# A score tile inside two dense chunks, the sums of one norm ahead of two casts, one turn of x sooner

## The chip, the cores and the metric

The kernel runs on one core of a Trainium2 chip. The metric is device time of one execution in microseconds (us). The core has a matrix engine (TensorE, PE; its weight loads are PEld), a vector engine (DVE), an activation engine (ScalarE, ACT), a general engine (GpSimd, POOL) and a sync engine (SP) that here only issues DMA. Each works off its own instructions in the order in which the program lists them, and waits where one of them needs another engine's result.

## The reference

The program is an attention with RMS-normalised q and k, followed by a mixture of experts with a dense part. Shapes: q, k, v are 8 x 12 x 448 x 64; the tokens are 3584 x 768, 8 experts, hidden size 512.

```python
q_n, k_n = rmsnorm(q, g_q), rmsnorm(k, g_k)          # x / sqrt(mean(x*x) + 1e-6) * g
attn = softmax(q_n @ k_n.T / 8); x = attn @ v        # x becomes 3584 x 768
y_dense = relu(x @ w1_dense) @ w2_dense
expert_idx = argmax(x @ w_gate); gate_w = softmax(x @ w_gate)[expert_idx]
y_moe = gate_w * (relu(x @ w1[expert_idx]) @ w2[expert_idx])
out = y_dense + y_moe
```

## The kernel before

The heads of one image are taken in three groups of four, so the attention has 24 groups g, three to an image; an image takes about 24 us, which is called a period here. For a group, DVE takes statistics of q and k (`stats`, L281), ACT squares the means (`means`, L288), POOL adds them to the sums of squares (`ss`, L290), ACT takes logarithm and exponential (`norms`, L294 and L296) and gets 1/rms as `r`. POOL multiplies q and k with it (`normalise`, L302, four instructions that write `xn`) and casts v (`values`, L267, two casts that write `va`). PE transposes `xn` into the two banks of the PSUM tile `W` (`transposes`, L313, 28 of them) and DVE copies them out (`qT`, `kT`).

Scores come in seven tiles per group (`scores`): PE multiplies into a PSUM tile `sc` (L348), of which there are two, and ACT takes the exponential (L350, an "exp"). The products with v are L366 (`AV`), and DVE divides them (L393). Once a group's x is there, PE turns it (`xtrans`, L407), DVE copies it (`xturned`, L413), and PE makes the router's logits from it (L425).

When an image's x is complete, its dense layer follows in four chunks m of 128 tokens (`dense`, L616, six matmuls each with 512 columns, the last chunk in halves) during the next period. A chunk lands in bank 0 or bank 1 of `W`, the same banks that the transposes L313 write, and ACT empties it with a relu (`relu`, L624). Its records go to memory with an indirect DMA that POOL issues (`scatter`, L488). POOL also issues the loads of the experts' weights (L680); SP issues the loads of q, k and v (L235, L261), and a load into a staging buffer waits until POOL has read what was there.

The order of all this is a table, `AT`: each step gets a time in units of a seventh of a group, `attention` sorts all steps by it, and the steps are written out in that order. A time says nothing but where a step stands among the others; on each engine the instructions run in that order. Steps from unit 161 on stand in a list of their own, `AT['tail']`, which also has the turns of gathered tokens and the loads of expert numbers into PE's registers (`number`, L847).

In the attention `s1` to `s6` are the times of the score tiles, with one entry for each of the three groups of a period; `me` is that of `means`, which puts L288 on ACT and L290 on POOL; `de` holds the dense chunks, in pieces of the six matmuls.

After the attention (from about 205 us) PE works through expert tiles, with two matmul stages each, and the outputs go out by indirect DMA.

## Time and profile before

| | us |
|---|---|
| median of 3 runs | 353.22 |
| the three runs | 355.0, 351.29, 353.22 |
| the profiled execution | 350.3 |
| its span | 348.6 |
| PE, busy (share of the span) | 312.8 (90%) |
| DVE | 231.4 (66%) |
| ACT | 212.8 (61%) |
| POOL | 202.2 (58%) |

Shares are means over the whole span. In the attention, up to about 200 us, PE, DVE, ACT and POOL are each busy for eight to nine tenths or more of most slices; after it PE alone is. [...]

### The profile page before, as it was taken

Reading aid. Unit: us, or ns where it says so; the run is one execution under the profiler, and the core shown is the slowest. Engines: PE = TensorE matmul, PEld = TensorE weight load, DVE = VectorE, ACT = ScalarE, POOL = GpSimd, SP = SyncE. Lnnn points to the kernel's source line nnn. Section 1 sums busy time; section 2 is a strip of 40 time slices with the busy share of each in tenths; the row PEclk is TensorE's granted clock in tenths of the full one; section 3 lists DMA queues with packets and bytes.
Section 4 is the critical chain, followed back from the end, with each engine's and each line's share of the span. In section 5 each row is a group of like instructions: output and inputs, shape, how many; then the busy total and the mean of one; then the engine's idle time right before and its main releaser. Section 6 shows DMA issues by size and latency. Waiting matters only on the chain. (4 is left out here: it accounts for less than half of the span.)

```text
span 348.6 us, 11328 instructions
## 1 busy us (share of the span) xinstructions
PE 312.8 (90%) x4164; PEld 192.7 (55%) x4164; DVE 231.4 (66%) x835; ACT 212.8 (61%) x348; POOL 202.2 (58%) x290
## 2 busy tenths in 40 slices
PE   0389989989989899999899899999999999999990
PEld 0255656656656565666666556555555555555550
DVE  5988998878988879888898744258222226364641
ACT  2389998898898898998988834322332332323220
POOL 4666887788886987988987522462323221322222
PEclk9999999999999999999999999999999999999997
DMA  7999999999997999989999799999999948495422
GB/s 263 265 249 240 311 291 210 289 259 323 233 305 240 256 300 253 285 227 253 262 276 192 166 186 182 259 282 248 176 248 240 212 121 205 123 182 140 123 93 80
DMA packets 83406, 78.85 MB, mean 226 GB/s; under 512 B 46894, under 2 KB 76088, under 8 KB 83344
## 3 DMA queue, kind: packets, MB, share of 16 engines
q1 hardware_dynamic: 69360, 42.58, 50.8%
q0 software_dynamic: 13984, 35.47, 40.5%
q8 instruction: 36, 0.59, 0.7%
q14 instruction: 26, 0.21, 0.2%
HBM read 61.40 MB, written 23.02 MB: 242 GB/s over the span
## 5 line engine op out<-in xcount | busy, mean ns | idle before, releaser
L350 ACT ACTIVATE xflat<-sc 128x896 bf16<-128x896 f32 x168 | 143.8, 918 | 6.0 <-PE sc L348 5.4
L302 POOL TENSOR_TENSOR xn<-we,r 128x448 bf16<-128x448 f32 x90 | 82.0, 945 | 14.5 <-issue 6.8
L348 PE MATMUL sc<-qT,kT 64*128 64x448 bf16 (+1 forms) x384 | 65.9, 372 | 12.0 <-ACT xflat L350 8.8
L366 PE MATMUL AV<-va,xflat 128*128 128x65 bf16 (+1 forms) x1536 | 75.7, 195 | 0.5 <-ACT xflat L350 0.4
L281 DVE BATCH_NORM_STATS2 st<-we 128x6 f32<-128x128 f32 x336 | 70.3, 280 | 2.9 <-DMA we<-in_k_dram 2.8
L366 PEld LDWEIGHTS <-xflat 128*128 128x128 bf16 (+1 forms) x1536 | 59.9, 98 | 22.2 <-issue 12.1
L929 POOL DMA_INDIRECT out_dram<-xflat,tail x22 | 22.7, 1032 | 64.5 <-DVE xflat L928 52.4
L928 DVE COPY xflat<-yp 128x768 f32<-128x768 f32 x22 | 21.0, 956 | 46.3 <-PE yp L898 46.3
L878 ACT COPY heT<-AV 128x512 bf16<-128x512 bf16 x26 | 15.2, 585 | 55.3 <-PE AV L874 55.3
L488 POOL DMA_INDIRECT records<-rall,slot x32 | 33.1, 1036 | 23.7 <-ACT rall L624 18.0
L616 PE MATMUL W<-wd,xT 128*128 128x512 bf16 (+1 forms) x240 | 42.8, 339 | 0.7 <-DVE kT L334 0.7
L898 PE MATMUL yp<-we,heT 128*128 (+1 forms) x232 | 42.5, 326 | 0.0
L348 PEld LDWEIGHTS <-kT 64*128 64x128 bf16 (+1 forms) x384 | 24.1, 97 | 28.3 <-issue 22.0
L393 DVE TENSOR_TENSOR rall<-AV,inv 128x256 bf16<-128x256 f32 x96 | 36.3, 420 | 1.7
L859 PE MATMUL W<-we,xflat 128*128 (+1 forms) x132 | 32.6, 379 | 0.3 <-issue 0.2
L624 ACT ACTIVATE rall<-W 128x512 bf16<-128x512 f32 (+1 forms) x40 | 20.3, 509 | 19.9 <-PE W L616 18.4
L887 PE MATMUL yp<-wd,xflat 128*128 128x384 bf16 x176 | 32.2, 327 | 0.0
L864 ACT ACTIVATE hs<-W,tail 128x512 bf16<-128x512 f32 x26 | 17.9, 687 | 23.1 <-PE W L859 19.5
L898 PEld LDWEIGHTS <-heT 128*128 128x128 bf16 (+1 forms) x304 | 22.5, 97 | 15.0 <-issue 1.0
L267 POOL CAST va<-we 128x448 bf16<-128x448 f32 x48 | 26.9, 593 | 0.0
L616 PEld LDWEIGHTS <-xT 128*128 128x128 bf16 (+1 forms) x240 | 16.8, 102 | 15.3 <-issue 4.4
L887 PEld LDWEIGHTS <-xflat 128*128 128x128 bf16 x176 | 16.9, 98 | 14.1 <-issue 1.3
(151 smaller groups left out, 348.6 us busy)
## 6 DMA issues: line engine op xcount, KB each, us to landing
we<-in_moe_w_dram POOLq DMA_DIRECT2D x16, 768.0 KB, 10.0
we<-in_q_dram SPq DMA_DIRECT2D x24, 448.0 KB, 9.6
we<-in_k_dram SPq DMA_DIRECT2D x11, 896.0 KB, 8.2
we<-in_v_dram SPq DMA_DIRECT2D x48, 128.0 KB, 9.6
we<-in_v_dram SPq DMA_DIRECT2D x48, 96.0 KB, 7.2
wd<-in_moe_w_dense_dram POOLq DMA_DIRECT2D x2, 768.0 KB
we<-in_k_dram SPq DMA_DIRECT2D x2, 448.0 KB, 3.5
records<-rall,slot POOLq DMA_INDIRECT x32, 6.6
```

The source lines that it names most:

```text
L267: nc.gpsimd.tensor_copy(vas[g % 3][:, :, :, a * 32:a * 32 + 32].rearrange("p s h i -> p h s i"), xin["v", g].rearrange("p h (s i a) -> p h ...
L281: return [lambda s=s: nc.vector.bn_stats(sts[g][:, "qk".index(name), s].rearrange("p h c -> p (h c)"), xin[name, g].rearrange("p h (s d) - ...
L302: (eng or nc.gpsimd).tensor_tensor(xn[name, g][:, :, hh], xin[name, g][:, hh].rearrange("p (s d) -> p s d", d=D), r[:, "qk".index(name), : ...
L348: nc.tensor.matmul(ps[out, hh, :S], kT[row, w:w + out.stop - out.start], qT[row, r], start=True, stop=True, skip_group_check=True)
L350: nc.scalar.activation(x, ps[:, :, :S], AF.Exp, scale=scale)
L366: on("AV", nc.tensor.matmul(av[:, hh, m], exs[g, s][rows_, hh, QC[m]:QC[m] + P], va[rows_, s, hh, :De], start=(first and s == full[0] and ...
L393: on("AV", nc.vector.tensor_tensor(x[:, 2 * hh + r], av[:, hh, :, :D].rearrange("p m (a i) -> p m a i", a=2), inv[:, hh].unsqueeze(3).to_b ...
L488: i = nc.gpsimd.indirect_dma_start(out=rec, out_offset=bass.IndirectOffsetOnAxis(ap=slot[b % 2][:, m:m + 1], axis=0), in_=rb[b % 3][:, m], ...
L616: on("W", nc.tensor.matmul(o, xTs[b][:, kk, q0:QC[m] + P], wd1[:, kk, c], start=(kk == 0), stop=(kk == KD - 1), skip_group_check=(m == 3)) ...
L859: got = [nc.tensor.matmul(he[c], xRs[t][:, kk, c], matrix(t, 0, h, kk * F, (kk + 1) * F), start=(kk == 0), stop=(kk == KD - 1)) for h, c i ...
L887: nc.tensor.matmul(yps[t][:, dd, :HD], xRs[t][:, KD + i], wd2[:, i, dd * HD:(dd + 1) * HD], start=(i == 0), stop=False, skip_group_check=True)
L898: return [nc.tensor.matmul(yp[c, dd, :HD], heTs[t][:, i, c], matrix(t, 1, h, cols.start, cols.stop), start=False, stop=(i == FT - 1), skip ...
```

## The change

Three numbers of the table change, the third dense chunk is cut in two, and one step gets a time of its own.

```diff
- 'me': [2.591, 2.79, 3.569],
+ 'me': [1.6, 2.79, 3.569],
...
-        (2, 0, [(20.56, 0, 6)], 20.943, 27.29), (3, 0, [(26.48, 0, 6)], 28.824, 32.5)],
+        (2, 0, [(20.56, 0, 2), (20.62, 2, 6)], 20.943, 27.29), (3, 0, [(26.48, 0, 6)], 28.824, 32.5)],
...
  'sx': {(5, 3): 155.2},
+ 'xs': {22: 160.9},
...
- 's0': [-0.586, 0.455, 2.566],
+ 's0': [-0.586, -0.4, 2.566],
...
- 's3': [0.9, 0.991, 3.16],
+ 's3': [0.65, 0.991, 3.16],
...
- 'tail': [('tu', 0), ('tu', 1), ('tu', 2), ('nu', 0), ('nu', 1), ('xt', 22), ('de', 6, 2), ('de',
+ 'tail': [('tu', 0), ('tu', 1), ('tu', 2), ('nu', 0), ('nu', 1), ('de', 6, 2), ('de',
...
-            put1(at("xt", z, g), ("xt", g), xtrans, g)
+            put1(AT["xs"].get(g, at("xt", z, g)), ("xt", g), xtrans, g)
```

What this does to the engines' order, at the three places where it matters. Line numbers of the changed kernel are one higher from the new row of the table on.

PE, third dense chunk of the first image (a period near 64 us; `xT_81` is that image's x, `kT_92` the keys of a group, `wgb` the router's weights):

```order
L366 MATMUL AV<-va_93,xflat 128x65
L616 LDWEIGHTS xT_81
L616 MATMUL W<-wd_88,xT_81 128x512
...
L425 LDWEIGHTS xT_82
L425 MATMUL AV<-wgb,xT_82 128x8
...
L348 LDWEIGHTS kT_92
L348 MATMUL sc<-qT,kT_92 128x448
```

```order
L617 LDWEIGHTS xT_81
L617 MATMUL W<-wd_88,xT_81 128x512
L349 LDWEIGHTS kT_92
L349 MATMUL sc<-qT,kT_92 128x448
L349 LDWEIGHTS kT_92
L349 MATMUL sc<-qT,kT_92 128x448
L617 LDWEIGHTS xT_81
L617 MATMUL W<-wd_88,xT_81 128x512
```

Before, the six matmuls of the chunk stood together, and the logits and then two score tiles followed. Now two of the six come, then the first of those score tiles (two matmuls), then the other four, the logits, and the second score tile. In the second chunk likewise a score tile (the one in quarters, of four matmuls), which stood behind all six, stands behind two of them. Both hold in six periods.

ACT, first period with a dense part, from the first relu on (`m` is the square, `xflat<-sc` an exp):

```order
L624 ACTIVATE rall<-W 128x512
L350 ACTIVATE xflat<-sc 128x896 x2
L624 ACTIVATE rall<-W 128x512
L350 ACTIVATE xflat<-sc 128x896 x2
L288 ACTIVATE m_1471<-st 128x28
```

```order
L625 ACTIVATE rall<-W 128x512
L351 ACTIVATE xflat<-sc 128x896 x3
L625 ACTIVATE rall<-W 128x512
L351 ACTIVATE xflat<-sc 128x896
L289 ACTIVATE m_1471<-st 128x28
```

One exp has moved ahead of the second relu, and in the same way one moves ahead of the third; the squares keep their place among the exps.

POOL, second period with a dense part (`va_94` is the cast of v, `ss` the sum that needs ACT's square, `rall` a record):

```order
L302 TENSOR_TENSOR xn<-we,r 128x7x64 x4
L488 DMA records<-rall,slot_85 29824x648
L267 CAST va_94<-we 128x2x7x32 x2
L290 TENSOR_TENSOR ss<-st,m_2287 128x28
L488 DMA records<-rall,slot_85 29824x648
L680 DMA we<-in_moe_w_dram 128x3x1024
```

```order
L303 TENSOR_TENSOR xn<-we,r 128x7x64 x4
L489 DMA records<-rall,slot_85 29824x648
L291 TENSOR_TENSOR ss<-st,m_2256 128x28
L268 CAST va_94<-we 128x2x7x32 x2
L489 DMA records<-rall,slot_85 29824x648
L681 DMA we<-in_moe_w_dram 128x3x1024
```

The sum has moved ahead of the two casts; this holds in six groups, five of them in periods with a dense part. The fourth piece of the change, at the end of the attention, moves the eight transposes L407 of group 22 on PE from behind logits, a product `AV` and two register loads (L847) to the place ahead of these. The orders of DVE and SP are the same as before.

## Rows read from the trace of the kernel before

**Rows 1.** Table by stretch, after the attention: us, then busy time of each engine.

```profile
240.00:260.00 20.00, 20.00 (x126) 11.47 (x125) 7.02 (x20) 6.36 (x10) 5.75 (x6) 1.00 1.04 235
```

**Rows 2.** Waits of the whole run: us in total, times, longest.

```profile
ACT rall L624 <- PE W L616: 18.4, 22, 2.7
...
PE sc L348 <- ACT xflat L350: 8.8, 20, 1.0
```

**Rows 3.** Timeline of PE, period from 76 us: start, duration, [idle before <-releaser].

```profile
83.07 1.47 PE L616 MATMUL W<-wd,xT 128*128 128x512 bf16 x6
...
86.34 0.35 PE L348 MATMUL sc<-qT,kT 64*128 64x448 bf16 x1
...
89.15 1.47 PE L616 MATMUL W<-wd,xT 128*128 128x512 bf16 x6
90.46 0.34 PE L425 MATMUL AV<-wgb,xT 128*128 128x8 bf16 x8
...
92.11 0.36 PE L348 MATMUL sc<-qT,kT 64*128 64x448 bf16 x2
...
99.33 0.37 PE L348 MATMUL sc<-qT,kT 64*128 64x448 bf16 x2 [0.52 <-ACT xflat L350]
...
100.23 0.58 PE L313 MATMUL W<-ident,xn 64*128 64x64 bf16 x28 [0.24 <-POOL xn L302]
```

**Rows 4.** Timeline of PE's weight loads behind the second chunk, same period.

```profile
84.47 0.11 PEld L348 LDWEIGHTS <-kT 64*64 64x64 bf16 x4 [0.42 <-issue]
84.78 0.10 PEld L348 LDWEIGHTS <-kT 64*128 64x128 bf16 x2 [0.20 <-issue]
...
85.22 0.44 PEld L313 LDWEIGHTS <-xn 64*128 64x128 bf16 x26 [0.33 <-issue]
```

**Rows 5.** Timeline of ACT, same period.

```profile
84.58 0.60 ACT L624 ACTIVATE rall<-W 128x512 bf16<-128x512 f32 x1 [0.77 <-PE W L616]
...
86.66 0.25 ACT L288 ACTIVATE m<-st 128x28 f32<-128x28 f32 x1
86.79 0.93 ACT L350 ACTIVATE xflat<-sc 128x896 bf16<-128x896 f32 x1
...
91.15 2.53 ACT L350 ACTIVATE xflat<-sc 128x896 bf16<-128x896 f32 x3
93.55 0.26 ACT L288 ACTIVATE m<-st 128x28 f32<-128x28 f32 x1
```

**Rows 6.** Timeline of POOL, same period.

```profile
88.31 3.64 POOL L302 TENSOR_TENSOR xn<-we,r 128x448 bf16<-128x448 f32 x4 [1.07 <-ACT r L296]
...
93.18 1.14 POOL L267 CAST va<-we 128x448 bf16<-128x448 f32 x2
...
94.69 1.01 POOL L488 DMA_INDIRECT records<-rall,slot  x1 [0.17 <-issue]
...
96.50 3.67 POOL L302 TENSOR_TENSOR xn<-we,r 128x448 bf16<-128x448 f32 x4
```

**Rows 7.** Timeline of ACT, the same place one period later.

```profile
117.67 0.26 ACT L288 ACTIVATE m<-st 128x28 f32<-128x28 f32 x1
...
119.58 0.32 ACT L294 ACTIVATE ln<-ss,eps_t 128x28 f32<-128x28 f32 x1 [0.84 <-POOL ss L290]
```

**Rows 8.** Timeline of POOL there.

```profile
118.17 1.17 POOL L267 CAST va<-we 128x448 bf16<-128x448 f32 x2
...
120.74 3.64 POOL L302 TENSOR_TENSOR xn<-we,r 128x448 bf16<-128x448 f32 x4
```

**Rows 9.** Timeline of PE: the third transposes of that period and of the next.

```profile
124.94 0.58 PE L313 MATMUL W<-ident,xn 64*128 64x64 bf16 x28
...
149.19 0.58 PE L313 MATMUL W<-ident,xn 64*128 64x64 bf16 x28 [0.33 <-POOL xn L302]
```

**Rows 10.** Timeline of PE at the end of the attention.

```profile
205.31 0.62 PE L407 MATMUL W<-ident,rall 128*128 128x128 bf16 x8 [0.82 <-issue]
```

**Rows 11.** Waits of SP's DMA queue.

```profile
SPq L261 <- POOL ss L290: 14.4, 8, 4.8
```

## The prediction

> **What bounds the kernel now.** I read the table by stretch first. After the attention PE has no gap: 20.00 of 20 us [rows 1]. So whatever PE loses or gains before that point reaches the end unchanged, and only the attention has to be worked out. There the table of waits shows where the edits aim: ACT stands 18.4 us before relus, waiting for dense chunks, and PE stands 8.8 us for a score buffer that ACT has not emptied yet [rows 2]. A score tile inside the chunk gives ACT an exp to do during the first wait, and that could shorten the second.

> Next I followed one period on four engines. It closes in a ring. PE's second dense chunk and the transposes behind it set when ACT can take the next exps; behind these ACT makes the `r` of one group; that releases POOL's multiplication for this group at 88.31; from there POOL works almost without a gap through records, casts, sum, records, a weight load and the third group's multiplication, until 100.17 [rows 6]; and PE's transposes of the third group wait for that last one, 0.24 us here and 0.33 us two periods on [rows 3, 9]. I call these the third transposes. So in these periods POOL, not ACT, has the last word: PE's wait of 0.52 us for ACT at 99.33 [rows 3] costs little, since without it PE would only stand longer at the third transposes.

> **Second chunk: a tile inside it.** Before, the weight loads behind the chunk are those of the tile in quarters (84.47), of one more tile (84.78), and then of the transposes, of which the first two go through and the others are held, with a gap of 0.33 us, until 85.22 [rows 4]. The relu ran from 84.58 to 85.18 [rows 5]: it empties the bank into which the second transpose writes. So the two tiles cost PE nothing there; they fill the time in which the transposes wait for the relu.

> With the quarter tile inside the chunk, the chunk ends later, so the relu ends later, and the transposes with it. The tile itself takes 0.31 us (84.47 to 84.78) [rows 4]. To it comes the change from full-height to half-height matmuls and back. From the start of six dense matmuls to the next work it is 1.40 us where a half-height tile follows (83.07 to 84.47) and 1.31 us where full-height logits follow (89.15 to 90.46) [rows 3, 4], so one change costs 0.09 us. The way back has no row of its own; its bounds are 0 and, as for the way there, 0.09, and I take 0.09. Insertion: 0.31 + 0.18 = 0.49 us.

> [...]

> What follows from the 0.49 us: the next score pair, whose second matmul ended at 86.34 + 0.35 = 86.69, ends at 87.18, and its exp, at 86.79 before, can start at about 87.2, 0.4 us later, although ACT is there sooner [rows 3, 5]. Logarithm and exponential for `r` stand behind that exp in ACT's order. So POOL's start of 88.31 becomes 88.7, and its first records end at 93.6 instead of 93.18.

> **Third chunk: a tile inside it, and the sum ahead of the casts.** PE arrives 0.49 us later and now has two more changes of height before the score tile of 92.11, which comes at 92.11 + 0.49 + 0.18 = 92.78. The tile itself costs nothing extra, because it only changes places with the rest of the chunk. This score tile feeds the last exp before the square: it is ready at 92.78 + 0.36 = 93.14, an exp takes 0.8 us in a row of three (91.15 to 93.55), so the square starts at 93.95 and ends at 94.2, where before it ran from 93.55 to 93.81 [rows 5].

> POOL now has the sum ahead of the casts. POOL is free at 93.6, but the sum needs the square: it starts at 94.3. Before, casts (1.14), sum and a gap (0.17) took 1.51 us from 93.18 to the records at 94.69, so a sum takes 0.20 us. Everything on POOL's queue stands behind it: the casts start at 94.5, and behind them there is no sum any more, so the records come 1.14 + 0.17 us later, at 95.8 to 95.85, against 94.69: 1.15 us late [rows 6]. The weight load and the third group's multiplication follow without a gap, so the third transposes move from 100.23 by up to 1.15 us. If the square were no later than before, the sum would end at 94.15 and the records would come at 95.45, 0.75 us late. Middle of the two: **+0.95 us for this period, and the same for its twin at 149.19** [rows 9]: +1.9 us.

> **Where the sum's move is meant to help.** One period later the square (117.67 to 117.93) is there before POOL reaches the casts at 118.17, and behind casts and sum ACT stands 0.84 us before its logarithm [rows 7, 8]. That wait goes. But POOL's multiplication for the third group ends at 120.74 + 3.64 = 124.38, and comes 0.4 us later by its later start; the third transposes stand at 124.94 [rows 8, 9], so they can come at about 124.85: −0.1 us, although ACT gains more. The two remaining periods with third transposes lie between this one (−0.1) and the twins (+0.95). They do not wait for POOL today, so I take them below the middle, +0.35 each: +0.7 us.

> **The rest.** The sixth period with a dense part has no third transposes; there PE just carries the 0.49 us: +0.5. The turn of group 22 puts 0.45 us of transposes (205.31 to 205.76, when the next chunk begins) ahead of the register loads instead of behind them, and with them the gap of 0.82 us [rows 10]. What follows is ready in both cases. If the gap stays as long behind the new neighbour, nothing is won; if the loads run during the transposes, 0.45 us. I take 0, since the same 32 product instructions stand right before the loads in both orders. SP and DVE keep their orders, and each score tile, cast and sum takes as long as before.

> **Sum:** 1.9 − 0.1 + 0.7 + 0.5 + 0 = **+3.0 us**. On the profiled execution of 350.3 us that is 353.3 us. The median of the runs shown is 353.22 us, 2.9 us above the profiled execution, and the changed kernel will be judged beside such runs: **356.2 us**. With the low ends (0.75 for the twins, −0.1 for the two others, −0.45 for the turn) the sum is 1.5 − 0.1 − 0.2 + 0.5 − 0.45 = +1.25; with the high ones (1.15; 0.95 for the others) 2.3 − 0.1 + 1.9 + 0.5 = +4.6.

> **Rivals.**
> - *ACT's lead counts, POOL does not hold the transposes.* Then the two waits of rows 2 shrink as meant. Worked out: the stands for a score buffer, at most 8.8 us in all of which some 5 lie in these periods, go, and twelve insertions cost 12 × 0.18 = 2.2: about −3 us, 350.2. For it: a tenth of that 18.4 us of ACT's waiting suffices. Against it: POOL's gapless stretch of rows 6 and both waits of rows 3 and 9. Chance 0.12.
> - *Nearly nothing.* The square comes early enough that POOL does not stand, and PE's later chunks are swallowed by the waits for ACT that follow (0.52 us each period). Then only the last period's +0.5 and a few tenths remain: 353.5 to 354. For it: PE's waits are there to swallow it; against it: the square of 93.81 against POOL at 93.18 [rows 5, 6]. Chance 0.26.
> - *Worse: loads come late.* The casts empty the staging of v; SP's loads of v wait on POOL there already, 14.4 us in 8 waits [rows 11], and q and k queue behind them. If a cast 1.3 us later makes the next multiplication wait for data, five periods lose up to 1.3 us in place of the terms above: 5 × 1.3 + 0.5 = +7, 360. It decides once POOL's first multiplication waits for a load and not for `r`. Against it: SP has long idle waits. Chance 0.10.

> The forecast keeps 0.52.

> **Range and chances.** A run of this kernel varies by 1 to 2 us, so about 1% (3.5 us) is what can be told from no change: the borders are 349.7 and 356.75. Forecast and high ends reach past the upper one in some four tenths of their cases: 0.52 × 0.4 = 0.21, with the last rival 0.30 for slower. Half of the first rival and a little of the second lie below the lower one: 0.07 for faster. Within 1%: 0.63. The range takes in the second rival and the high ends with the spread of the runs: 352.0 to 358.8. Below it lies the first rival, above it the third, together about 0.2.

> **What the profile after would show.** The relu of the second chunk ends half a us later and the transposes' row behind it grows or starts later; ACT's waits before second and third relu shrink to a tenth or two. POOL has a wait "sum for square" of 0.5 to 0.8 us in at least three periods, and PE's waits at the third transposes grow from 0.24 and 0.33 to near 1 us and appear in other periods. ACT's wait before the logarithm (0.84) is gone. At the end the gap of 0.82 us stands before a dense chunk. I am wrong if the third transposes come sooner relative to the period's start, if the sum finds its square done, or if the transposes behind the second chunk are not held by its relu.

## The result, and the profile after

The changed kernel takes **356.87 us** (median of 5 runs, 355.07 to 358.94) beside 353.22 us before in the same session. The ratio is **1.0129, with a 95% interval of 1.0093 to 1.0166**, some 4.5 us; the two medians alone differ by 3.65. I had forecast 356.2 us from a sum of +3.0 us, and had given 0.63 to a change of less than 1% and 0.30 to slower. The median lies just outside that 1%, whose upper border was 356.75 us.

The profiled execution is the longest of the five: 358.94 us, span 357.2 us, mean granted clock 0.978. The one before had a span of 348.6 us and 0.993. Of these 8.6 us some 2 are thus this execution's own, and 2.9 come from the one before, which took 350.3 us against a median of 353.22. Executions that the comparison counts as disturbed are left out of every ratio below, so that two kernels (e3, e4) have a trace but no ratio, and the traces of e3, e4, e5, e8 and e9 are of such executions. In those five traces PE waits for a DMA behind the attention, once or twice for 4.4 to 7.5 us, and it is 150.5 to 161.2 us from the dense chunk that follows the attention to the end, against 142.1 to 144.1 in the other eight; up to that chunk they are held against the others below.

The table of waits after, the lines that answer to [rows 2], and POOL's and the third transposes' beside them (us in total, times, longest):

```profile
ACT xflat L351 <- PE sc L349: 18.2, 39, 1.2
...
POOL xn L303 <- ACT r L297: 12.0, 8, 2.1
ACT rall L625 <- PE W L617: 9.0, 8, 2.7
PE sc L349 <- ACT xflat L351: 6.5, 16, 0.8
...
PE W L314 <- POOL xn L303: 3.8, 5, 1.0
```

ACT's waits before its relus halved and PE's for score buffers shrank from 8.8 to 6.5 us, as the edit intends. But the time came back in other rows. ACT's waits for scores were 5.4 us before, POOL's for `r` 2.8, and PE's at transposes for POOL's product 1.3.

The second chunk of the period from 76 us on PE, to hold against [rows 3, 4]:

```profile
83.56 0.39 PE L617 MATMUL W<-wd,xT 128*128 128x512 bf16 x1
84.10 0.38 PE L349 MATMUL sc<-qT,kT 64*64 64x448 bf16 x4
84.41 1.04 PE L617 MATMUL W<-wd,xT 128*128 128x512 bf16 x4
85.38 0.36 PE L349 MATMUL sc<-qT,kT 64*128 64x448 bf16 x2
85.58 0.19 PE L314 MATMUL W<-ident,xn 64*128 64x64 bf16 x1
86.14 0.56 PE L314 MATMUL W<-ident,xn 64*128 64x64 bf16 x27 [0.36 <-issue]
```

(The second matmul of the first row has no record.) From the chunk's start to the relu it was 1.51 us [rows 3, 5]; now it is 85.49 − 83.56 = 1.93. The insertion costs 0.42 us, and the transposes stand 0.36 us for the relu. ACT at the same place, against [rows 5]:

```profile
85.49 0.60 ACT L625 ACTIVATE rall<-W 128x512 bf16<-128x512 f32 x1
85.98 0.91 ACT L351 ACTIVATE xflat<-sc 128x896 bf16<-128x896 f32 x1
86.78 0.24 ACT L289 ACTIVATE m<-st 128x28 f32<-128x28 f32 x1
87.64 0.92 ACT L351 ACTIVATE xflat<-sc 128x896 bf16<-128x896 f32 x1 [0.61 <-PE sc L349]
88.45 0.31 ACT L295 ACTIVATE ln<-ss,eps_t 128x28 f32<-128x28 f32 x1
88.79 0.23 ACT L297 ACTIVATE r<-ln 128x28 f32<-128x28 f32 x1
```

ACT is earlier at its work, but the exp at 87.64 has to wait 0.61 us for scores that PE makes 0.42 us later. The logarithm and `r` stand behind this exp in ACT's order. This wait of 0.6 us is there in all six periods. POOL behind it, against [rows 6]:

```profile
89.15 3.64 POOL L303 TENSOR_TENSOR xn<-we,r 128x448 bf16<-128x448 f32 x4 [1.80 <-ACT r L297]
...
94.51 0.24 POOL L291 TENSOR_TENSOR ss<-st,m 128x28 f32<-128x28 f32 x1 [0.51 <-ACT m L289]
94.70 1.11 POOL L268 CAST va<-we 128x448 bf16<-128x448 f32 x2
95.97 1.00 POOL L489 DMA_INDIRECT records<-rall,slot  x1 [0.16 <-issue]
96.97 0.82 POOL L681 DMA_DIRECT2D we<-in_moe_w_dram  x1
97.79 3.65 POOL L303 TENSOR_TENSOR xn<-we,r 128x448 bf16<-128x448 f32 x4
```

The sum waits 0.51 us for its square, with casts, records, weight load and the third multiplication behind it. Against the start of the second chunk the records come 12.41 us in place of 11.62, 0.79 us later. And PE at the third transposes, against the end of [rows 3]:

```profile
100.27 0.37 PE L349 MATMUL sc<-qT,kT 64*128 64x448 bf16 x2 [0.65 <-ACT xflat L351]
100.57 0.36 PE L426 MATMUL AV<-wgb,xT 128*128 128x8 bf16 x8
101.50 0.58 PE L314 MATMUL W<-ident,xn 64*128 64x64 bf16 x28 [0.57 <-POOL xn L303]
102.01 0.68 PE L349 MATMUL sc<-qT,kT 64*64 64x448 bf16 x6
102.62 2.00 PE L367 MATMUL AV<-va,xflat 128*128 128x65 bf16 x29
```

The last row took 1.39 us before (from 101.35 us). The table by stretch shows why it takes 2.00 (busy time of each engine, and behind POOL's the granted clock as a share of full speed):

```profile
100.00:101.00 1.00, 0.65 (x10) 0.36 (x9) 0.06 (x2) 1.00 (x3) 1.00 (x2) 1.00 1.01 266
101.00:102.00 1.00, 0.50 (x28) 0.47 (x28) 0.97 (x4) 0.96 (x3) 1.00 (x3) 1.00 1.11 240
102.00:103.00 1.00, 1.00 (x22) 0.59 (x17) 0.93 (x4) 0.56 (x1) 0.89 (x3) 0.90 1.09 219
103.00:104.00 1.00, 1.00 (x19) 0.82 (x17) 0.93 (x5) 1.00 (x2) 0.93 (x1) 0.50 1.13 232
...
106.00:107.00 1.00, 0.81 (x13) 0.52 (x13) 0.00 (x0) 0.92 (x2) 1.00 (x2) 0.89 0.64 217
```

Behind two stands (times in which PE idles) of 0.65 and 0.57 us the granted clock falls to 0.50 for 3.4 us (102.8 to 106.2 us); summed over the rows of the table, the two that are left out included, that is 1.71 us of clock lost. The same happens at 154 and at 205 us, for 3.4 us each. In the trace before, the granted clock is 1.00 throughout up to 343 us, and PE's last work starts at 339.15 us. What a fall costs can be read from the stretch from the third transposes to the second chunk: 6.96 us twice without one (76.60 to 83.56, 127.36 to 134.32), 8.26 and 8.20 with one. So **one fall costs about 1.25 us**, an estimate from these two. Nothing in my sum stands for it.

### The profile page after: what moved, and what is told of

The parts are those of the page before. It is cut to its first block, busy times and chain, and to the rows that moved or that the text cites. A ratio compares the mean times of both kernels' runs of the same rounds, so it can differ in the third digit from the quotient of the medians.

```text
span 357.2 us, 11293 instructions
## 1 busy us (share of the span) xinstructions
PE 313.7 (88%) x4129; PEld 194.0 (54%) x4164; DVE 231.8 (65%) x835; ACT 216.5 (61%) x348; POOL 202.2 (57%) x290
## 5 line engine op out<-in xcount | busy, mean ns | idle before, releaser
L351 ACT ACTIVATE xflat<-sc 128x896 bf16<-128x896 f32 x168 | 146.0, 916 | 19.9 <-PE sc L349 18.2
L303 POOL TENSOR_TENSOR xn<-we,r 128x448 bf16<-128x448 f32 x90 | 82.0, 943 | 18.4 <-ACT r L297 12.0
L367 PE MATMUL AV<-va,xflat 128*128 128x65 bf16 (+1 forms) x1536 | 79.0, 198 | 1.9 <-ACT xflat L351 0.4
L349 PE MATMUL sc<-qT,kT 64*128 64x448 bf16 (+1 forms) x384 | 69.0, 380 | 10.2 <-ACT xflat L351 6.5
L367 PEld LDWEIGHTS <-xflat 128*128 128x128 bf16 (+1 forms) x1536 | 62.5, 99 | 24.9 <-issue 14.3
L860 PE MATMUL W<-we,xflat 128*128 (+1 forms) x121 | 30.5, 379 | 1.5 <-issue 0.7
```

The source lines that it names most:

```text
L303: (eng or nc.gpsimd).tensor_tensor(xn[name, g][:, :, hh], xin[name, g][:, hh].rearrange("p (s d) -> p s d", d=D), r[:, "qk".index(name), : ...
L349: nc.tensor.matmul(ps[out, hh, :S], kT[row, w:w + out.stop - out.start], qT[row, r], start=True, stop=True, skip_group_check=True)
L351: nc.scalar.activation(x, ps[:, :, :S], AF.Exp, scale=scale)
L367: on("AV", nc.tensor.matmul(av[:, hh, m], exs[g, s][rows_, hh, QC[m]:QC[m] + P], va[rows_, s, hh, :De], start=(first and s == full[0] and ...
L860: got = [nc.tensor.matmul(he[c], xRs[t][:, kk, c], matrix(t, 0, h, kk * F, (kk + 1) * F), start=(kk == 0), stop=(kk == KD - 1)) for h, c i ...
```

## The experiments

The traces are compared by the third transposes of every period (P1 to P5 are the five periods from one to the next), and by the stretch from the last of them to the next dense chunk after the attention. A star marks a fall of the clock in the stretch.

| kernel | P1 | P2 | P3 | P4 | P5 | sum | sum less 1.25 per fall | last stretch |
|---|---|---|---|---|---|---|---|---|
| before | 24.93 | 24.23 | 24.71 | 24.25 | 24.14 | 122.26 | 122.3 | 32.43 |
| after | 25.18 | 24.90 | 25.86* | 25.95 | 25.57* | 127.46 | 125.0 | 34.22* |
| e1 sum alone | 25.05 | 24.79 | 25.51* | 24.89 | 24.03 | 124.27 | 123.0 | 33.73* |
| e2 second chunk alone | 25.05 | 24.56 | 25.06 | 24.59 | 24.48 | 123.74 | 123.7 | 34.18* |
| e3 third chunk alone | 25.22 | 24.22 | 24.72 | 24.26 | 24.15 | 122.57 | 122.6 | 33.89* |
| e9 turn alone | 24.72 | 24.22 | 25.15 | 24.92 | 24.24 | 123.25 | 123.3 | 32.45 |
| e5 after, sum put back | 25.04 | 24.56 | 25.07 | 24.60 | 25.70* | 124.97 | 123.7 | 32.72 |
| e4 after, r early | 25.18 | 26.35* | 24.11 | 25.01 | 24.31 | 124.96 | 123.7 | 32.12 |
| e8 before, r early | 24.41 | 24.73 | 24.41 | 24.52 | 24.39 | 122.46 | 122.5 | 32.43 |
| e7 e5, r early | 23.97 | 24.27 | 24.00 | 24.07 | 24.10 | 120.41 | 120.4 | 32.23 |
| e10 second chunk, r early | 24.51 | 24.73 | 24.28 | 24.67 | 25.04 | 123.23 | 123.2 | 34.16* |
| e11 third chunk, r early | 24.64 | 24.63 | 24.48 | 24.54 | 24.94 | 123.23 | 123.2 | 34.22* |

In P1 to P5, e9 has the order of the kernel before. Its 1.0 us more (in P3 and P4, with stands of 0.27 and 0.30 us that the trace before lacks) say how far one trace can be trusted: sums that differ by less than 1 us are not told apart by the sums alone, and what a smaller difference comes from has to be read from the rows. In e6 the third transposes stand elsewhere, so it has no row here.

**The sum alone (e1).**

```
- 'me': [2.591, 2.79, 3.569],
+ 'me': [1.6, 2.79, 3.569],
```

> Only the norms' sum of one group in three goes ahead of the two casts; PE's order stays as before. Theory A (POOL's lateness reaches PE as a stand at the third transposes): the sum waits 0.4 to 0.6 us for its square in the twin periods, the casts come behind it, and the third transposes come 0.5 to 0.8 us later there; the period with the 0.84 us wait before the logarithm gives 0.1 back: +0.5 to +1.5 us against before. Theory B (only what is put into PE's chunks costs): 0. Theory C (the whole loss is the granted clock that falls behind longer stands of PE): 0 where no stand passes half a us, else about 1.25 us for each fall.

Measured: ratio **1.0096** (1.0057 to 1.0136), some 3.4 us. POOL's wait is there, and the stands at the third transposes with it:

```profile
94.14 0.24 POOL L290 TENSOR_TENSOR ss<-st,m 128x28 f32<-128x28 f32 x1 [0.72 <-ACT m L288]
...
97.43 3.65 POOL L302 TENSOR_TENSOR xn<-we,r 128x448 bf16<-128x448 f32 x4
```

```profile
99.52 0.37 PE L348 MATMUL sc<-qT,kT 64*128 64x448 bf16 x2 [0.52 <-ACT xflat L350]
99.82 0.36 PE L425 MATMUL AV<-wgb,xT 128*128 128x8 bf16 x8
101.14 0.58 PE L313 MATMUL W<-ident,xn 64*128 64x64 bf16 x28 [0.96 <-POOL xn L302]
```

The five periods grow by 0.8 us without the fall; P2 and P4, the twins, by 0.56 and 0.64 us. That is theory A's figure, and far less than 3.4. (P4 of e9 is as long without the sum's move, so it is the rows above that show the wait, not the lengths.) The rest is the clock. The seven executions behind the ratio had lost 4.9 to 8.2 us of clock each (one less the mean granted clock, times the span; median 6.3), against 1.4 to 4.6 in the kernel before (medians of 2.6 to 3.0 in three sessions, the program's end included, where PE has nothing to do). By estimate the difference of some 3.5 us is two falls of 1.71, at 1.25 us each 2.5 us. 0.8 and 2.5 make 3.3 of the 3.4. Theory B falls. Theory C has the larger part right, but not the whole: the stands that the sum's wait makes cost time of their own.

**The tile in the second chunk alone (e2).**

```
- 's3': [0.9, 0.991, 3.16],
+ 's3': [0.65, 0.991, 3.16],
```

> Only the quarter score tile goes inside the second dense chunk, six times. Theory A: 0.42 us on PE each time, as in the changed kernel's trace; the exp that stands ahead of the logarithm on ACT then waits for its scores, so POOL's multiplication starts 0.3 us later against the chunk; stands at the third transposes of 0.3 to 0.7 us in the twins: +2.5 to +3.5 us, and 1.25 more for each fall of the clock. Theory B: 6 x 0.42 = +2.5 us, stands at the third transposes no longer than before (0.24 and 0.33). Theory C: 0, or a multiple of 1.25 us.

Measured: ratio 1.0038 (0.9998 to 1.0079), median loss of clock 2.5 us, as before. The five periods grow by 1.5 us, and the last stretch by 0.5 beside its fall: 2.0 us of waits, against 1.3 measured, whose interval reaches from 0 to 2.8 us.

```profile
100.36 0.37 PE L348 MATMUL sc<-qT,kT 64*128 64x448 bf16 x2 [0.53 <-ACT xflat L350]
100.65 0.36 PE L425 MATMUL AV<-wgb,xT 128*128 128x8 bf16 x8
101.22 0.58 PE L313 MATMUL W<-ident,xn 64*128 64x64 bf16 x28 [0.21 <-POOL xn L302]
```

The stands at the third transposes are 0.21 and 0.24 us, where they were 0.24 and 0.33. POOL's multiplication starts 0.35 us later against the second chunk, but PE arrives later by as much (0.33 us). So theory B is right for this edit, though not in its size of 2.5 us: PE pays for it itself, 0.33 to 0.35 us in each of P2 to P5.

**The tile in the third chunk alone (e3).**

```
- (2, 0, [(20.56, 0, 6)],                  's0': [-0.586, 0.455, ...
+ (2, 0, [(20.56, 0, 2), (20.62, 2, 6)],   's0': [-0.586, -0.4, ...
```

> Only the score tile goes inside the third dense chunk, six times (and the tile ahead of the logits in the turns without a chunk). All theories: 0.05 us on PE each time, as in the changed kernel's trace, +0.3 us. Theory A adds that ACT's exps before the square of the third group come earlier, which POOL, late by itself, does not use: -0.3 to +0.5 us against before. If ACT's lead counts, -1 to -2 us.

Measured: no ratio. In the trace the five periods grow by 0.3 us, but not as expected: all of it is in P1, and P2 to P5 are within 0.01 us of before. No wait shrinks either: PE still stands 0.52 us for ACT ahead of the third transposes in each.

**The changed kernel with r early (e4).**

```
- 'no': [3.342, 3.796, 4.041],
+ 'no': [3.342, 3.796, 3.691],
```

> The changed kernel, and on ACT the logarithm and the exponential for r of one group in three go ahead of the one exp that waits 0.6 us for its scores there; nothing else moves. Theory A: POOL's multiplications start some 0.8 us earlier in every period, the stands at the third transposes (0.96, 0.57, 0.48 and 0.93 us) shrink to 0.3 or less, and the falls of the granted clock behind them go: 3 to 5.5 us less than the changed kernel, -1 to +1.5 us against before. Theory B: as the changed kernel, +4 to +5 us against before. Theory C: 1.25 us less for each fall that goes, at most 3.75 us less than the changed kernel.

Measured: no ratio. The trace shows half of it. POOL's multiplication starts 1.06 us sooner against the second chunk, and yet the third transposes stand:

```profile
88.78 3.64 POOL L303 TENSOR_TENSOR xn<-we,r 128x448 bf16<-128x448 f32 x4 [0.74 <-ACT r L297]
...
95.19 0.24 POOL L291 TENSOR_TENSOR ss<-st,m 128x28 f32<-128x28 f32 x1 [1.57 <-ACT m L289]
```

```profile
102.18 0.58 PE L314 MATMUL W<-ident,xn 64*128 64x64 bf16 x28 [0.95 <-POOL xn L303]
```

POOL spends what it gains waiting 1.57 us for the square. So theory A's expectation failed in three of four places: stands of 1.14, 0.95 and 1.06 us remain, and only the one of 0.48 us shrinks, to 0.15. That points to the place of the sum and not to POOL's late start, and suggested to put the sum back.

**The changed kernel with the sum put back (e5)**, that is with `'me': [2.591, ...`:

> The changed kernel with the norms' sum back behind the two casts; both score tiles stay inside their chunks. Theory D (formed after the sum alone and the tiles alone): the stands near 1 us at the third transposes come from the sum that waits for its square, and the falls of the granted clock come behind such stands; the second chunk's tile costs PE 0.42 us each time, the third's 0.1. Then no stand at the third transposes is over 0.4 us, the clock falls no oftener than before, and the time is 2 to 3 us over before. Theory A as in the prediction (POOL's later start after the second chunk holds the third transposes): stands of 0.5 to 0.9 us stay in three or more periods, +3.5 to +4.5 us.

Measured: ratio 1.0084 (1.0036 to 1.0132). The stands at the third transposes are those of before:

```profile
101.22 0.47 PE L314 MATMUL W<-ident,xn 64*128 64x64 bf16 x20 [0.24 <-POOL xn L303]
...
150.89 0.81 PE L314 MATMUL W<-ident,xn 64*128 64x64 bf16 x28 [0.34 <-POOL xn L303]
```

The loss of clock falls from a median of 6.0 us (five executions of the changed kernel, 4.3 to 7.9) to 3.2 (eleven, 1.4 to 3.9). Theory D's mechanism holds: the sum's move brings both stands and falls (one fall, at 151 us, is left in the trace's five periods, behind stands of 0.52 and 0.34 us). The cost that stays is the tiles', 3.0 us with an interval of 1.3 to 4.6, where the trace's periods say 1.5.

**The third transposes later (e6)**: e1, and the transposes behind the quarter tile, another pair and 16 products.

```
- 'tr': [2.755, ...   'tq': [3.163, ...   'tk': [3.197, ...
+ 'tr': [3.855, ...   'tq': [3.885, ...   'tk': [3.915, ...
```

> The kernel before, with the sum ahead of the casts, and PE's third transposes put behind the quarter score tile, another pair and 16 products, about 1.4 us of PE's work that waits for nothing of POOL's (DVE's evictions follow them). Theory D: the stands of 1.13, 0.96, 0.38 and 1.06 us that the sum made disappear, and with them the falls of the granted clock in the middle of the attention; the one at the attention's end can stay. Within 0.3% of before, 2 to 4 us under the sum alone. If the falls don't hang on the stands: two or more falls, as with the sum alone, and +0.6 to +1%.

Measured: ratio **1.051** (1.0424 to 1.0596). Neither theory's number came. The stands at the transposes are gone, but the next pair of scores now waits for what DVE copies out of them, and two more stands moved together:

```profile
79.71 0.37 PE L348 MATMUL sc<-qT,kT 64*128 64x448 bf16 x2 [0.53 <-ACT xflat L350]
80.00 0.36 PE L425 MATMUL AV<-wgb,xT 128*128 128x8 bf16 x8
80.51 0.38 PE L348 MATMUL sc<-qT,kT 64*64 64x448 bf16 x4 [0.15 <-ACT xflat L350]
81.32 0.36 PE L348 MATMUL sc<-qT,kT 64*128 64x448 bf16 x2 [0.43 <-ACT xflat L350]
...
86.13 0.55 PE L348 MATMUL sc<-qT,kT 64*128 64x448 bf16 x2 [1.31 <-DVE kT L332]
```

The experiment did not take the stands away, so it does not part the two theories. It shows something else: at the pair of 0.53 and 0.43 us (with a stand of 0.15 us between) the clock fell in four of five periods (at 82, 137, 164 and 191 us; the first of these stays at 0.50 for 10.2 us). So a fall needs no stand at the third transposes; these came at other stands close together.

**r early without the sum's move (e7), and on the kernel before (e8).**

> The changed kernel with the sum back behind the casts, and on ACT the logarithm and r ahead of the exp that waits for its scores. Theory D: POOL starts 0.8 to 1 us earlier and no stand at the third transposes is left, but they were short without the sum's move: 0 to 1 us under the changed kernel without the sum's move, so +1 to +2.5 us against before. Theory A: 2 to 3 us under it.

> The kernel before, and on ACT the logarithm and r of one group in three ahead of the exp behind the second relu; nothing else. Both theories: the logarithm then waits 0.3 us for the sum, r comes 0.4 us earlier, the stands of 0.24 and 0.33 us at the third transposes go, the exp comes 0.9 us later: -1 to +0.5 us against before. It is the version that could beat both.

Measured: e7 **0.9945** (0.9907 to 0.9982), faster than both kernels; e8 1.0033 (0.9978 to 1.0088), no change. In e7 the period is 24.1 us, no fall is in its attention, and the median loss of clock is 2.1 us:

```profile
100.80 0.36 PE L349 MATMUL sc<-qT,kT 64*128 64x448 bf16 x2 [0.31 <-ACT xflat L351]
101.10 0.36 PE L426 MATMUL AV<-wgb,xT 128*128 128x8 bf16 x8
101.67 0.58 PE L314 MATMUL W<-ident,xn 64*128 64x64 bf16 x28 [0.22 <-POOL xn L303]
```

The stand for ACT is 0.31 to 0.43 us in these periods, in place of 0.52. That beats both theories' expectations, in which the tiles were a cost only. In e8, PE stands 0.57 to 0.61 us for a score buffer behind the second chunk in every period and still 0.53 ahead of the third transposes: with r early the exp comes later on ACT, and PE waits for it.

**One tile and r early (e10, e11), and the turn alone (e9).**

> The kernel before with the quarter tile inside the second chunk and the logarithm and r ahead of the exp. With the roots early and no tile inside a chunk, PE stood 0.57 us for a score buffer behind the second chunk and 0.53 us ahead of the third transposes in every period. If the quarter tile's early exp is what ends the first of these: that 0.57 us goes, the tile costs 0.42, so 0 to -0.2 us a period: 0 to -1 us against before. If PE only pays for the tile: +2 us against before.

> The kernel before with the tile inside the third chunk and the logarithm and r ahead of the exp. If this tile's early exp is what shortens the wait ahead of the third transposes (0.53 to 0.31 us where both tiles and the early roots were together): -0.1 to -0.3 us a period, while the 0.57 us behind the second chunk stay: -0.5 to -1.5 us against before. If the two tiles only pay together: 0 to +0.5 us.

> Only the turn of group 22 comes sooner: its eight transposes stand among the last products instead of behind the gap of 0.82 us. From the lengths of the attention's last stretch in the runs so far (with and without the turn moved): 0.4 us less from the last third transposes to the next dense chunk, because the gap stays and the 0.45 us of transposes then fill time in which PE stood for ACT or run earlier. By the prediction: 0. Against before: -0.4 to 0 us, not to be told from nothing by the whole time; the trace decides.

Measured: 1.0026 (0.9992 to 1.0061), 0.9982 (0.9935 to 1.0029) and 1.0006 (0.9968 to 1.0043), no change each. With one tile the stands of e8 stay in part: e10 keeps 0.52 to 0.57 us ahead of the third transposes, e11 the 0.57 to 0.61 behind the second chunk and 0.37 to 0.53 ahead of the third transposes. Only both tiles and r early together (e7) bring the stand ahead of the third transposes to 0.31 to 0.43 us in every period and leave, behind the second chunk, just the 0.36 us for the relu. In e9 the transposes of group 22 take their 0.46 us among the products, and the gap of 0.86 us stands before the dense chunk; the last stretch is 32.45 us against 32.43. So the turn is worth nothing, as predicted, and not the 0.4 us of the expectation.

## Why the prediction came out as it did

**Direction and size.** +3.0 us was forecast, and some 4.5 were measured. That the median of 356.87 us lies within 1 us of the forecast is in part luck, since by the estimate below more than half of the measured loss is something for which my sum has no term. The changed kernel's five periods grow by 2.7 us without their falls, and the last stretch by about 0.5 us without its own, 3.2 together. But nearly 1 us of that is P4, where stands of 0.28 and 0.36 us for DVE's evictions came, and the square later by as much: P4 is 25.95 us, its twin P2 24.90. A stand of 0.30 us at the place of the first of these is in e9 too, where the order is the old one, so one trace does not show that P4's extra comes from the change; without it the waits are some 2.2 us. What the sum lacked was **the granted clock**: 6.0 us of it lost in the median execution, against 2.8 in the kernel before (median of another session). By estimate that is (6.0 − 2.8) / 1.71 = 1.9 falls and 1.9 × 1.25 = 2.4 us. 2.2 and 2.4 make 4.6; with the whole of P4 it would be 5.6, and the interval is 3.3 to 5.9. The step that failed is the first one, that whatever PE loses before the end of the attention reaches the end *unchanged*, by which I priced a stand by its length alone: behind stands of 0.65 and 0.57 us the granted clock was 0.50 for 3.4 us, and the 29 products there took 2.00 us in place of 1.39.

**Second chunk, 0.49 us.** Measured 0.42: the tile's 0.31 (84.10 to 84.41), and 0.11 that is left for two changes of height, by estimate 0.05 each where I took 0.09; no row shows a change by itself. That the relu comes later and holds the transposes is right (0.36 us). That this delays POOL is right too (0.35 us against the chunk's start, 0.4 forecast). That the third transposes then wait for POOL is wrong: e2 shows that PE is later by as much, so the cost lies on PE in nearly all periods (0.12 us in P1, 0.33 to 0.35 in P2 to P5) and not in the twins alone.

**Third chunk, 0.18 us.** From its first weight load to the start of the last chunk (the one in halves) it was 5.87 us and is 5.92: 0.05. In e3 even that is gone by the third transposes in four of five periods.

**The sum's move, most of +0.95 for each twin.** Right in its mechanism, and e1 shows it alone: 0.56 and 0.64 us. With the second chunk P2 grew by 0.67, less than forecast; only P4, by 1.70, brought the twins' sum above 1.9. The period with the 0.84 us before the logarithm: that wait is gone, and P3 is 0.1 us shorter without its fall (−0.1 forecast). P1 gained 0.25 and P5 about 0.2 us without its fall (0.35 each forecast).

**Sixth period +0.5, turn 0.** +0.5 without its fall, and 0 (e9).

**The rivals.** "ACT's lead counts" did not happen here, but e7 shows that the lead can count: with both tiles, r early and the sum in its old place the ratio is 0.9945. In the changed kernel the logarithm stands behind an exp that waits for PE, and the sum ahead of its square; e4 and e5, which mend one of these each, do not bring the lead out. "Nearly nothing" (353.5 to 354 us) is excluded by the interval. The loads of v did not come late: in the period from 76 us and in its twin POOL's first multiplication waits for `r` (1.80 us), not for a load. The fall of the clock was no rival of mine, though two stands within a microsecond, 0.52 and 0.24 us, stood in [rows 3].

**Open.** Why the clock falls behind some pairs of stands and not behind others. That the sum's move brings more falls is shown (after against e5: 4.3 to 7.9 us of clock lost against 1.4 to 3.9). Whether they would go if the stands alone went was tried once, in e6, and not settled. That the 2.4 us are falls of the attention is an estimate from the loss of clock of whole executions; the one trace of the changed kernel has three falls there.

## What to carry to other kernels

When work is put ahead of an engine's other work, look whether its input is there at that moment: the sum was moved 1 us ahead of work that was ready, in front of a square that was not, and everything behind it waited (0.51 us in the period from 76 us). A lead on one engine can be lost at the next engine of the ring: here two tiles cost 0.8% alone and gained 0.5% with a logarithm put ahead of one exp. And price a new stand of TensorE by more than its length: add the chance of a fall of the clock, which here cost about 1.25 us by the estimate above.
